# Last 128 tokens' values in two column halves, last transfers from two queues, low-word shift of the weights also on ScalarE, new order

## The chip, the cores and the metric

One core of one Trainium2 chip. The metric is the device time of one execution in microseconds (us): 916.03 us, the median of 3 runs (915.87 to 916.19).

The engines in the tables: PE is TensorE's matmul, PEld its weight load, DVE is VectorE, ACT is ScalarE, POOL is GpSimd, SP is SyncE, which here issues nearly all transfers. The names of lines (L459) are lines of the kernel before.

## The reference

Threshold attention, then a channel mix of the RWKV kind, all in fp32. There are 8 batches of 576 tokens, 8 heads of 64, so a model width of 512; the hidden width is 1024.

```python
scores = q @ k.T / 8
scores = where(scores >= max(scores) - tau, scores, -1e9)
x = softmax(scores) @ v                      # heads side by side: [8, 576, 512]
xk = mu_k * x + (1 - mu_k) * x_prev          # x_prev: the token before, zero at the start
xr = mu_r * x + (1 - mu_r) * x_prev
k = relu(xk @ w_k)                           # 512 -> 1024
out = sigmoid(xr @ w_r) * ((k * k) @ w_v)    # 1024 -> 512
```

q, k and v are fp32. The three weight matrices come as 64-bit floats, which the kernel takes as pairs of 32-bit words.

## The kernel before, in words

**An order written down.** The kernel first lists 5,647 steps. `add` records for each its engine, a cost, the code that issues it, and which buffers (or regions of them) it reads and writes. Some steps have alternatives on another engine (`alt`); the string `PICKS` says, step by step, which is taken. The table `PLACES` then gives every step its place in one global order, two digits for each. `follow` reads it and picks buffer slots; `issue` emits the steps in that order. Each engine runs its own steps in the order in which they were emitted, and semaphores hold a step until what it depends on is done. A step that waits therefore holds all later steps of its engine.

**Attention.** Per batch there are four pairs of heads; a pair of heads is a job (batch 0's jobs come in two halves). A job works in units of 128 query rows. Per unit and head PE writes the scores of 576 keys into PSUM (L628, L639, L656), DVE takes the maximum (L740), the threshold is made of it on ACT, DVE or POOL (L748, L756, L761), ACT takes the exponential (L768), DVE masks and sums (L776), DVE inverts the sum (L801), and ACT or POOL scales (L816, L812). The result is turned, by PE and an eviction from PSUM (L830, L845 on ACT, L846 on DVE) in the first two batches, by DVE and transfers after (L865, L878). Then PE multiplies with v (L1017), and an eviction puts x into place. For full precision operands are split into a high and a low part, and three products are summed.

**Weights.** There are 20 pieces of 128 x 512 (8 of w_k, 4 of w_r, 8 of w_v). `weight` turns the 64-bit words of a piece into fp32 and splits it, in the midst of the attention of the first batches. A piece takes a transfer (L435), a clamp of its high words on POOL (L444), a scaled copy on ACT (L451), then three steps on DVE that join in the low words' top bits: a shift right by 29 into a PSUM buffer (L459), sign bits joined to that (L467), and the final join (L477). A copy on ACT or POOL (L487, L491) and a difference on POOL (L496) make the two parts. The PSUM buffer is one of four of the tag `w`, which PE's matmuls and transposes use too.

**Mix.** `ffn_chunk` handles 256 tokens: 16 chunks of a batch's own (main) and 2 of four batches' last 64 tokens (end). It mixes neighbours, multiplies with w_k (L1211), applies relu and squares (L1219, L1220, L1224 or L1234, L1243), multiplies with w_r (L1262), takes the sigmoid through tanh (L1266, L1270 or L1273), multiplies with w_v (L1285), takes the product of both on DVE (L1291), and sends the rows out (L1301). The value product runs over two tiles of 128 tokens, each 8 slices of the hidden width with three matmuls of 512 columns. The last thing that the kernel does is the second such tile of the last end chunk: a product of 128 x 512, and two transfers of 64 rows each, both from SP.

```python
            add(
                "DVE",
                0.6,
                lambda j=j, vps=vps: V.tensor_tensor(sg.get()[:, j], vps.get(), sg.get()[:, j], op=ALU.mult),
                reads=[vps],
                writes=[(sg, j)],
                key=key - 20,
            )
            n = P // len(rows[j])
            for y, dst in enumerate(rows[j]):
                add("DMA", DQ, lambda j=j, y=y, dst=dst, n=n: SY.dma_start(dst, sg.get()[y * n : (y + 1) * n, j]), ...)
```

Of the kernel before, what the change touches and what calls it, by code (L numbers as in the profile page):

```python
# [22 lines left out]
    "!(!!!$!#!+!,!o%x!*!)!%!&!1!=!r!}$0$C$>$G$^%C%m!.!c!n#)#1#=#E#H!w#g$U&)&9&](Z(t!2!]#G#Q#a#w$M&>!0#b&4(*(9(B(S(~#+#m#v",  # L23
    "&p&y(%(z)+!`&Q)&)1)H)^*,*7#@$B(`(b(p({*(*A#L$;)w*4*D*N*T*b%[&J)s)f)y*%*9*Z!f$)*B*S*d*n*v*{$E&~*Y*y*~+)+0+8$])j*x+.+3",
    "+A+K+R!e#>+G+E+T+e-<-H$?&[,|.1.A.N.q/$#4$F+p,C,Q,X.E/Y%d(0+c+[+o+|,*,=(l+`-a-N-i-u-~.)#Z.4/T/M/]/e/j/o*)-e0$0*060<0G",
    "0L!-!P#l!>!<!C!E!F!Q!?!A!B!D!S!V!x#!!_!k!X!q!^#&!T!O![!b!d!j!U!W!Y!a!l!~#3#8!s##!y#(#-#0#:#I#N#d#h#p!@#,$Z!i!m!p!u!t",
    "!z!v!|!{#%#*#D#M#O#<#B#6#J#T#[#$#.#/#7#2#9#5#C#;#F#W#}$1$:$!$+#j#s#R#Y$J$N$O$S$V$[!/!R%W#A#U#K#V#P#X#`#f#c#i#{#~$I$T",
    "#n#x$($5$2$@#r#_#z$%$#$-#e#q#k#u$8$=$z$~$g$x$,$<$`$c%,%2%4%F%K%c!Z#?&<#S#]#t$9$4#|#o$$$.$6#y$D$K$H$P$&$3$/$7$Y${%+%B",
    "$p$t$l%8$k$n$A$X$L$R$Q$W$b$i$h$o%b%o%|&!$r%$%&%:%=%N&,&/&1&6&:&K$_%3%U%g*K%9%I%V&c()(8(^)T)q(J(i)S){*0*6*=*F*L*Q*U*W",
    "*e+D+m+r,),1,4,:,k,o,r,{-:-@.:.T*@*J*O*]*a*g*q*z+,+w-k.v-v-z-}.+.U.^.c.e.m.w/</C+4+;+>+M+V*u*|+(+C+Q,Y/Q/_/b/h0P0^0b",  # L30
    "1E1L1_0y0}1%11191G1u1{2%2T$*$e(3$m$w$}%#%(%E%S%@%L$a$d$f$j$s$q$u%7%<%M%]%f&$%}%j%p%s$v$y$|%%%!%-%*%0%)%1%.%5%?%G%P%_",
    "%r&&%T%`&E&G%>%D%6%;%H%X%R%Y%A%O%J%Q%n%v&i&l%l%w%~&?%e%k&x(#(&(-(/(T(Y%/%h))%{&+&0&H&X&T&2&8&B%Z%^%a%i%u%q%z&C&N&R&`",
    "&Z&g&d&k&n&u%t%y&%&(&#&*&-&3&.&5&7&=&f($(1(6&A&U&M&_&h&t&;&@&F&I&D&S&L&V&P&Y&W&b&q&z(A(X&{(2&s&|(](d(o(s(y(|)%);)=&O",
    "(()z(.(5(<(C(H(M(=(W(e&^&a&e&j&r&w(+(Q(v)>)L(I).(n(E(K(L(4(7&m&o(>(D(F(N&v&}(!(,(m(u)#),(_(g(:(?(j(x(V(a(;(@(h(q(r)$",
# [263 lines left out]
def tile_threshold_attention_then_rwkv_ffn(  # L298
# [1153 lines left out]
```

## Time and profile before

| | us |
|---|---|
| median of 3 runs | 916.03 |
| the profiled execution | 915.72 |
| its span, first to last instruction | 914.00 |
| PE busy | 902.3 |
| DVE busy | 715.5 |
| POOL busy | 666.5 |
| ACT busy | 598.5 |

The span is that of one profiled execution; the time around it is 1.72 us. Busy time counts an instruction from its start to its end, and instructions of one engine overlap a little, so the sum of single durations is larger than the busy time. In the chain of waits each piece stands only for the time until the next piece takes over, so there a group's pieces are shorter than its durations. A share of busy time is a mean over stages with different limits.

### The profile page before, as it was taken

How to read it: one execution, taken by the hardware profiler on the slowest of the kernel's cores; microseconds unless marked ns; L12 is line 12 of the kernel's file. 1: busy time of each engine (PE TensorE's matmuls, PEld its weight loads, DVE VectorE, ACT ScalarE, POOL GpSimd, SP SyncE). 2: the span in 40 equal slices, each digit the busy share in tenths (PEclk: the TensorE clock that was granted, in tenths of full speed). 3: DMA queues.
4: the chain of work that ended last, by engine and by line, in shares of the span. 5: the costliest groups of instructions: out<-in, count | busy, mean ns of one | idle time of the engine just before them, and what ended most of it. 6: DMA issues, size and time to landing. Idle time of an engine off the chain costs nothing.

```text
span 914.0 us, 17624 instructions
## 1 busy us (share of the span) xinstructions
PE 902.3 (99%) x5970; PEld 744.1 (81%) x5970; DVE 715.5 (78%) x1615; ACT 598.5 (65%) x1154; POOL 666.5 (73%) x824
## 2 busy tenths in 40 slices
PE   8999999999999999999999999999999999999997
PEld 6677877797878887988887978888889888879986
DVE  7999999998878898988889988888888777701131
ACT  6789999778675767565755475757686666434211
POOL 1789988886774967786977686867687868577742
PEclk9999999999999999999999999999999999999999
DMA  8767333499989999899987979999898887630001
GB/s 332 276 217 246 105 106 119 145 305 308 334 296 311 313 320 322 301 323 313 299 297 272 315 252 321 305 321 320 296 321 291 281 310 261 238 131 24 24 24 23
DMA packets 146249, 226.60 MB, mean 248 GB/s; under 512 B 20080, under 2 KB 82672, under 8 KB 146160
## 3 DMA queue, kind: packets, MB, share of 16 engines
q1 hardware_dynamic: 146016, 225.49, 73.1%
q8 instruction: 47, 0.77, 0.4%
q14 instruction: 42, 0.34, 0.1%
q10 hardware_dynamic: 144, 0.00, 0.0%
HBM read 108.27 MB, written 73.14 MB: 198 GB/s over the span
## 4 chain that ended last, share of the span: by engine, by line
PE 84%; DVE 9%; ACT 4%; issue 1%; POOL 1%; ACTq 0%; DVEq 0%; POOLq 0%
PE w L1211 21%; PE w L1285 20%; PE w L1017 15%; PE s L656 12%; PE w L1262 9%; DVE p L776 3%; DVE sm L740 3%; PE s L628 3%; PE w L830 2%; PE s L639 2%; ACT p L768 2%; ACT pm L845 1%; DVE pt L865 1%; PE w L1378 0%; DVE r L1161 0%
## 5 line engine op out<-in xcount | busy, mean ns | idle before, releaser
L768 ACT ACTIVATE p<-s,sm 128x576 f32<-128x576 f32 x288 | 209.6, 738 | 122.8 <-DVE sm L740 100.0
L776 DVE SCALAR_TENSOR_TENSOR p<-s,sm,p 128x576 f32<-128x576 f32 x288 | 230.9, 811 | 32.4 <-ACT p L768 19.7
L740 DVE TENSOR_REDUCE sm<-s 128x1 f32<-128x576 f32 x288 | 213.2, 750 | 42.4 <-PE s L656 30.4
L1211 PE MATMUL w<-xk,wk 128*128 128x256 f32 x1728 | 227.5, 281 | 0.0
L1211 PEld LDWEIGHTS w<-xk,wk 128*128 128x128 f32 x1728 | 215.8, 188 | 4.1 <-issue 1.7
L1285 PE MATMUL w<-wv,k 128*128 128x512 f32 x864 | 218.0, 395 | 0.0
L1285 PEld LDWEIGHTS w<-wv,k 128*128 128x128 f32 x864 | 157.6, 188 | 31.2 <-ACT raw L529 0.4
L1017 PE MATMUL w<-pm,v 128*64 128x256 f32 (+1 forms) x1280 | 164.9, 409 | 0.0
L1017 PEld LDWEIGHTS w<-pm,v 128*64 128x64 f32 x1280 | 88.1, 137 | 64.0 <-issue 5.8
L865 DVE STREAM_TRANSPOSE pt<-p 128x1024 f32<-128x1024 f32 x96 | 117.8, 1228 | 8.0 <-POOL p L812 5.0
L812 POOL TENSOR_SCALAR p<-p,sm 128x576 f32<-128x576 f32 x119 | 89.2, 753 | 39.0 <-DVE sm L801 36.7
L1243 POOL TENSOR_TENSOR k<-r,k 128x512 fp32r<-128x512 f32 x72 | 93.0, 1294 | 31.0 <-ACT k L1224 28.4
L816 ACT ACTIVATE p<-p,sm 128x576 f32<-128x576 f32 x133 | 101.3, 771 | 20.2 <-DVE sm L801 19.8
L1262 PE MATMUL w<-wr,xk 128*128 128x512 f32 x432 | 112.4, 395 | 0.0
L656 PE MATMUL s<-st 128*128 128x288 f32 x480 | 107.9, 308 | 1.9 <-DVE p L776 1.6
L567 POOL TENSOR_TENSOR hl<-raw,hl 128x640 fp32r<-128x640 f32 (+1 forms) x64 | 97.9, 1539 | 14.3 <-ACT hl L550 7.8
L656 PE MATMUL s<-st,st 128*128 128x288 f32 x480 | 102.2, 296 | 0.0
L656 PEld LDWEIGHTS s<-st 128*128 128x128 f32 x480 | 78.3, 189 | 20.4 <-DVE p L776 8.3
L1262 PEld LDWEIGHTS w<-wr,xk 128*128 128x128 f32 x432 | 77.5, 188 | 13.8
L656 PEld LDWEIGHTS s<-st,st 128*128 128x128 f32 x480 | 77.2, 188 | 1.9
L1220 ACT ACTIVATE r<-r 128x512 f32<-128x512 f32 x72 | 45.4, 631 | 34.8 <-DVE r L1219 33.7
L1291 DVE TENSOR_TENSOR sg<-w,sg 128x512 f32<-128x512 f32 x36 | 24.0, 680 | 44.8 <-PE w L1285 40.9
(93 smaller groups left out, 1129.3 us busy)
## 6 DMA issues: line engine op xcount, KB each, us to landing
far<-pt SPq DMA_DIRECT2D x96, 576.0 KB, 4.2
pm<-far SPq DMA_DIRECT2D x48, 1152.0 KB, 7.3
st<-hl SPq DMA_DIRECT2D x64, 288.0 KB, 3.9
raw<-in_qk SPq DMA_DIRECT2D x28, 640.0 KB, 5.0
st<-hl SPq DMA_DIRECT2D x56, 256.0 KB, 3.8
v<-in_v SPq DMA_DIRECT2D x36, 320.0 KB, 4.0
st<-hl SPq DMA_DIRECT2D x64, 144.0 KB, 3.3
out<-sg SPq DMA_DIRECT2D x32, 256.0 KB, 4.0
```

Source lines behind the costliest of these rows:

```text
L567: lambda cs=cs: G.tensor_tensor(hl.get()[:, 1, cs], raw.get()[:, cs], hl.get()[:, 0, cs].bitcast(F32), op=ALU.subtract),
L656: PE.matmul(ss[y].get()[:, z, 0:HS], l.get()[:, c * P : (c + 1) * P], r[:, z * HS : (z + 1) * HS], start=(j == 0), stop=(j == 1),)
L740: lambda sv=sv, col=col: V.tensor_reduce(col(0), sv(), axis=AX.XY, op=ALU.max, negate=True),
L768: lambda sv=sv, pv=pv, col=col: A.activation(pv(), sv(), AF.Exp, bias=col(0)),
L776: lambda sv=sv, pv=pv, col=col: V.scalar_tensor_tensor(pv(), sv(), col(1), pv(), op0=ALU.is_ge, op1=ALU.mult, accum_out=col(2)),
L816: alt=[("ACT", 0.667, lambda y=y: A.activation(half(y), half(y), AF.Copy, scale=sm.get()[:, 3, y : y + 1]))],
L865: V.transpose(o, x)
L1017: PE.matmul(o[g].get()[hs, 0 : n[g]], vt.get()[:, c, hs], pt, start=(c == 0), stop=(c == 4))
L1211: PE.matmul(h.get()[:, f], l, r, start=(ct == 0 and i == 0), stop=(ct == NCT - 1 and i == 2))
L1243: lambda r=r, js=js: G.tensor_tensor(k2.get()[:, 1, js], r.get().rearrange("p (a b) -> p a b", a=2), k2.get()[:, 0, js].bitcast(F32), op=A ...
L1262: PE.matmul(z.get(), l, r, start=(ct == 0 and i == 0), stop=(ct == NCT - 1 and i == 2))
L1285: PE.matmul(vps.get(), l, r, start=(ft == 0 and i == 0), stop=(ft == NFT - 1 and i == 2))
```

## The change

1. The last end chunk's second tile is made in two halves of 256 columns, each with its own PSUM buffer, its own 24 matmuls, its own DVE product and its own two transfers of 64 rows by 256 columns. Of the second half, the second transfer is issued from ACT's queue instead of SP's.
2. The shift of the low words (L459) gets an alternative on ACT: a copy that reads the words as integers, multiplies by 2^-29 x 0.936 and writes an integer. `PICKS` takes it for 18 of the 20 pieces.
3. `PLACES` and `PICKS` are new throughout: another global order (5,658 steps), and other choices of engine for many steps. Thresholds go 93 to 65 on ACT, 117 to 142 on DVE and 78 to 81 on POOL; scalings go 133 to 119 on ACT and 119 to 133 on POOL.

```diff
 PLACES = (
-    "!(!!!$!#!+!,!o%x!*!)!%!&!1!=!r!}$0$C$>$G$^%C%m!.!c!n#)#1#=#E#H!w#g$U&)&9&](Z(t!2!]#G#Q#a#w$M&>!0#b&4(*(9(B(S(~#+#m#v",
...
 W_SCALE = 2.0**-112
+L_SCALE = 2.0**-29 * 0.936
...
             reads=[(words, 0)],
             writes=[bits],
             key=key,
+            alt=[("ACT", 0.57, lambda: A.activation(bu(), words.get()[:, :, 0], AF.Copy, scale=L_SCALE))],
         )
...
     def ffn_chunk(kind, b0, g, key):
+        final = kind == "end" and b0 + NTB == B
...
+            parts = 2 if final and j == 1 else 1
+            for part in range(parts):
+                fs = slice(part * DM // parts, (part + 1) * DM // parts)
+                vps = psum("w", [P, DM], 4)
+                for ft in range(NFT):
+                    w = pieces["v", ft, 0]
+
+                    def mm(ft=ft, w=w, vps=vps, ts=ts, fs=fs):
+                        wt, x = w.get(), k2.get()
+                        prods = [(x[:, 0, ft, ts], wt[:, 0, fs]), (x[:, 0, ft, ts], wt[:, 1, fs]), (x[:, 1, ft, ts], wt[:, 0, fs])]
+                        for i, (l, r) in enumerate(prods):
+                            PE.matmul(vps.get()[:, 0 : fs.stop - fs.start], l, r, start=(ft == 0 and i == 0), stop=(ft == NFT - 1 and i == 2))
...
+                    lambda j=j, vps=vps, fs=fs: V.tensor_tensor(sg.get()[:, j, fs], vps.get()[:, 0 : fs.stop - fs.start], sg.get()[:, j, fs], op=ALU.mult),
+                    reads=[vps] if parts == 1 else [vps, (sg, j)],
+                    writes=[(sg, j) if parts == 1 else (sg, (j, part))],
...
+                n = P // len(rows[j])
+                for y, dst in enumerate(rows[j]):
+                    eng, q = ("ACT", A) if part and y else ("DMA", SY)
+                    add(
+                        eng,
+                        DQ if eng == "DMA" else 0.55,
+                        lambda j=j, y=y, dst=dst, n=n, fs=fs, q=q: q.dma_start(dst[:, fs], sg.get()[y * n : (y + 1) * n, j, fs]),
```

## Rows read from the trace of the kernel before

**Rows 1.** The head of the page.

```profile
span 914.0 us, 17624 instructions
PE 902.3 (99%) x5970; PEld 744.1 (81%) x5970; DVE 715.5 (78%) x1615; ACT 598.5 (65%) x1154; POOL 666.5 (73%) x824
```

**Rows 2.** Busy time by stretch; columns as the first line names them.

```profile
core 0: us, PE busy (x) PEld busy (x) DVE busy (x) ACT busy (x) POOL busy (x), PEclk, DMA share, GB/s
0.00:57.10 57.10, 54.34 (x361) 39.23 (x362) 48.75 (x119) 41.83 (x94) 32.20 (x52) 1.00 0.80 292
57.10:169.30 112.20, 109.77 (x803) 86.06 (x802) 109.30 (x257) 104.99 (x237) 98.44 (x120) 1.00 0.46 151
169.30:800.00 630.70, 628.84 (x4169) 525.00 (x4168) 537.05 (x1191) 418.58 (x767) 470.69 (x582) 1.00 0.89 298
800.00:914.00 114.00, 109.38 (x645) 93.79 (x643) 20.37 (x52) 33.14 (x56) 65.20 (x72) 1.00 0.14 44
```

**Rows 3.** Chain of waits, 57.1 to 169.3 us: shares; pieces (start, us, what).

```profile
by line: DVE sm L740 10.9%; DVE p L776 10.4%; PE w L1017 9.7%; PE w L830 9.2%; ACT p L768 8.1%; PE s L656 7.5%; ACT pm L845 7.2%; PE w L1211 4.5%; issue 4.4%; PE w L1285 3.7%; DVE w L467 3.3%; DVE xT L477 3.3%; DVE w L459 3.2%; PE s L628 2.
...
68.42 0.18 ACT sm L748
...
71.48 0.56 ACT xT L451
...
102.59 0.60 DVE w L459
...
111.35 0.14 DVE sm L756
...
116.23 0.66 ACT p L816
...
120.97 0.58 ACT xT L451
...
142.12 0.23 DVE pm L846
```

**Rows 4.** Chain of waits at the end, from 881 us (start, us, what).

```profile
881.35 9.87 PE w L1211 x84
...
898.23 11.16 PE w L1285 x48
909.39 0.02 issue
909.41 0.69 DVE sg L1291
```

**Rows 5.** Instruction groups, shapes apart: busy us, mean ns, idle before.

```profile
L1219 ACT ACTIVATE r<-w 128x512 f32<-128x512 f32 x49 | 29.1, 593 | 28.3 <-PE w L1211 26.5 <-POOL k L1243 1.5
L1291 DVE TENSOR_TENSOR sg<-w,sg 128x512 f32<-128x512 f32 x36 | 24.0, 680 | 44.8 <-PE w L1285 40.9 <-ACT sg L1270 3.8
L451 ACT ACTIVATE xT<-wk 128x512 f32<-128x512 f32 x8 | 5.5, 681 | 0.0
L1039 DVE TENSOR_TENSOR xT<-w,xT 128x256 f32<-128x256 f32 x8 | 3.4, 420 | 0.0
```

**Rows 6.** Timeline at the end: SP's last output transfers (start, us).

```profile
908.09 3.15 SPq L1301 DMA_DIRECT2D out<-sg  x4
```

**Rows 7.** Timeline of the first 14 us: start, us, engine and line.

```profile
0.73 0.40 ACTq L379 DMA_DIRECT2D small<-in_tau  x1
...
9.11 0.50 ACT L529 ACTIVATE k<-k,small 128x256 f32<-128x256 f32 x1
...
13.22 0.99 PE L639 MATMUL s<-k 64*128 64x288 f32 x3 [0.29 <-DVE p L776]
```

**Rows 8.** DMA issues: count, KB of each, median us to landing.

```profile
out<-sg SPq DMA_DIRECT2D x32, 256.0 KB, 4.0
...
out<-sg SPq DMA_DIRECT2D x8, 128.0 KB, 3.1
xk<-in_qa SPq DMA_DIRECT2D x2, 448.0 KB, 7.3
...
k<-in_qa SPq DMA_DIRECT2D x1, 448.0 KB, 4.8
```

**Rows 9.** Busy time from 450 to 500 us.

```profile
450.00:500.00 50.00, 48.62 (x321) 39.89 (x320) 44.22 (x104) 29.08 (x55) 36.65 (x47) 1.00 0.89 301
```

More of the change, by code (lines that the diff above doesn't have):

```diff
@@ new lines @@
+    "0m!.!S#O!;!=!>!D!A!E!C!G!H!T!U!X!c!o!_!g![!l!e#-!V!R!^!f!d!i!W!Y!Z!b!k!m!v!~!|#,!t!w!x#!#2#4#9#G#J#d!?#($Q!h!n!p!r!s",
+    "!y!u!}!{#$#7#T$)$,#M#X#i#s#<#]###)#+#6#.#8#3#D#:#E#H#b$&$.#g#j#m#y#k#x$3$5$E$J$L$S!<#U%X#A#Q#I#R#N#V#a#e#f#l$-$D$P$Z",
+    "#r#z$+$>$/$9#t#`#}$%$$$0#h#n#o#u$I$g$n%%$f$u$k$y$R$m%2%4%G%J%P%Z!]#%&A#*#;#B#F#p$4#Y#C#S$:#|$B$G$F$K$*$7$2$<$T$t%.%>",
+    "${%#$q$|$^$b$A$U$H$O$M$X$a$j$h$o%d%t%y%|%*%9%&%5%C%O&-&0&4&:&<&O$Y%@%M&G(^%[%i&V&`&q&z(/(p*U(&)*)O)u*&*+*-*9*F*H*M*O",
@@ new lines @@
+    "*Y+S+v,),2,6,:,m,p,v,w,z-D-r-z.#*Z*_*h*l*o*q*t*v+)+G.6.E-S-X-}.!.*.,...7.N.d/,/1+>+A+K+Q+h*~+(+9+H+Y1&/H/L/d/l0c0u1$",
+    "131U1h0{1?1D1p1v2%2*202K2Z#w$V(6$l%!$r%,$s%A%T%F%L$_$c$e$i$v$p$w%:%<&P&X%h&%%w%W%u%n$~%$$x$z%)%/%0%7$}%-%(%1%K%Q%V%e",
+    "&!&+&H&L%Y%_%?%D%8%;%H%S%U%a%B%N%I%R&)&3&W&d%p%x%v%~%l%q&}(#()(+(1(h(l%3%g)7%}&*&8&I&a&Y&2&9&N%]%b%c%k%s%r%z&&&,&?&D",
+    "&v(;(A&x&|(.%m%{&$&(&#&1&/&7&.&6&5&=&E&c(:(C&b&o&^&f&T&Z&K&M&@&C&S&_&]&e&J&Q&R&[(@(Q(Y(a&r&w(B(T&m&s(q(u(w),)0)<)>&U",
@@ new lines @@
+    "(0)t(5(?(H(I(=(V(N(D(]&g&h&k&{($(%(,(3(Z(o(z(G(b(e)$)2)-(4(7&n&y(<(K(F(M(!(-(*(2(t)A)F)J(j(y(J(O(_(~(S(W(9(>([(m(f(s",
+    "(E(P(L(R)&);)M)Z):)?)6)E)P)V)`*;*1(d)9+{)C)K)[)c)S)k)])N)h(`(c(g(n(x(v({)T)a){*!)X)o)m)}*6*2(})#)%)+)()1)/)5).)4)3)B",
+    "*%*/*Q*T)D)H)U)s*B*E)=)@)I)Q)R)n)^)q)Y)_)d)i***0*R*]*7*<*C*K*j*w+d,*+|-b*.,@,c,k,s-M-p.X/>/h/}1b2G2j0_111Y1l2^2{3&3*",
+    "353R3j3p3}4/464831323@3U3_3e3i3n4?4B4E4K2P2T2V2`2c2e2i2t2x33373K2l2o2r3$303F3J3W3Z3b3f3k3A3M3t3x3~4O4i5(565U5Y4T4s4y",
@@ new lines @@
+    "5!5/5=5C5G5l684Y4_4n595K5Q5V5]5f5m)y*g-a+#+F+T+O+s+n+f+i+`)r)v)z)~*4*,*5*a+$+M+]+t+e+b+x+u*=*?*#*3*D*W*P*X*>*I*G*N*d",
+    "*i*m*s*y+&+3+[+++6*b*e*V*[*p*z*x+%*c*{*n*|+;+D+^+l,/,;+y,%,.,4,F,b,Z+/+1+,+5+4+=+?+L+:+C+B+I+_+k+}+q,=,?,,,0,9,J+W+Z",
+    "+P+X+a+p+j+r+g,!,+,1,H,N,R,],Y,_,h,x,g,t-*-L,$,W/=,d,|-,-.,n-B-G-P-V+~,&,(,-,7,5,<,G,O,S,i-9-7,}-2--,>,A,B,E,D,K,L,Q",
+    ",I,T,P,U-!-0-6-=-@-H-F-O-Q-Y,a,e,[,`,j,q,r,y,f,o,l,u-5-8->-E-Z-c-`-h-R-e.H.c.Z,~-#-%-(-&-1-/-4-+-:-3-;-A-J-W-d-s-~-w",
@@ new lines @@
+    "./-k-o-<-?-I-N-C-K-U-]-T-_-[-g-m-x.%-{.2.O.1.@.=.A.|/:-^.80l.M.i._.}.w/6/%.V/+-l-q-v.$.3.+.4.?.C.F.a.p.r.`.n/&-f-i.&",
+    ".(-n-y-u-|.-.9.5.;.K.Q.U.T.e.t.g.k.o/3.<.>.B.G.D.I.L.S.J.R.].f.s.v/$.z/5/S/D/I/;/B/~050>.Y.^.u.y.b.j.h.l/!/-/(/./9/F",
+    "/J/O/[/c/Y/u/X/].m.q///2.x.~/#/*/7/@/E/K/R/V/a/Z/k0&/i/p/v/y020@/C/x2I0!0+03040,0a0]0e0w/8/</A/G/M/N/W/o0*0I0Z151,0X",
+    "0v0t/_/b/Q/T/e/q/j/r/`/f/g/m0$0(0:000B0J0G0S0F0H/z/|/s/w0#0/0-01/{0%07090=0A0D0C0K0P0`0p0N0U1P1o1}0<0?0O0R0E0M0L0Q0T",
@@ new lines @@
+    "0[0Y0b0h0|1%1#1;1e1-171:1M0V0W0q0s0^0g0d0i0x0}0~1(1L1T1s1`1~2+1g1j1{22272u2J2n4[5E6)3!3T3v3z4>4U4q5;5>4e4l4r5%6_6b6j",
+    "6n6q6y6z72777>7B7F5p5t636=6@6C6H6M6Q6X6^6c5h5j676I6R6Z6t767M7Q7X7]6e6i6w7#7(7,7C7O7j7t7y7~7G7J7Y7_7f7.7:7?7T7[7}828G",
+    "8K8P8T8j8q8~9*9G8-888>8B8]8a8g8u9/9i4R5P5a6$7|8D5g6B7a7e8&819!9;9T868A8Q8k9h9p:0:2:4:C:F:N:R:X:]:f9%9(9+919495989=9D",
+    "9V9W9g:+:7:<:A:H:K:`:a:m:s:y;#9.9f9m9t9x9{9~:#:-:1:::@:[:r:};(;3:U:d:i:w;0;w;7;;;[;^;j;|<#<0<L<r;1;n;t<-<8<=<C<J<]<c",
@@ new lines @@
+    "0;0k5&191E1N1y1]212<25280j0n0o0r0z0y1!1*1.10161@1=2k1d1t2U2N3%1)1+12181/141>1A1<1C1B1F1I1Q1[1^1f1n1r1J1O1G1H1R1_1V1a",
+    "1K1W1S1Z1w1z2&2$2,2>2B3+1i1k1c1m1q1|1x2#1u2(2!2)2.2=2@2D2W2d2g2-2/2426232;2:2A292E2?2F2M2Q2]2S2v2|3#3G4.5*4u4I1X2C65",
+    "2_3]2s3o2q3a3{3w4$2O2Y2[2a2m2h2p363B3E3L3V3S534}4f4Q5)4W2H2L2w2~2R2b2X2f3(3.3-343:3<3D3?3^3I3h2y2z3;3=2}3,3)3/3C3O3H",
+    "3P3`4%4,4)47454:4^38393c3d3>3N3Q3X3l3r3s3y4(4+41444G4=4P3Y3[3|4!3g3q3m3u4-4342494D4F4Z4d4o4t4w5@5w6V6A6}4<4j834~5.5H",
@@ new lines @@
+    "5W5y5S5[5`5u4#4&4*404@4;4A4C4a4|5+57516D6?6v6J60714H4J4L4M4N4X4V4]4S4b4`4g4v4z555,5A5L5M5-544c4h585?5<5D4k5#4x5$5_5q",
+    "5{5s6%6+6-6d4m4p5J5O4{50525:5T5^5Z5b5i5k5o5x6!5}6&5n5r5B5F5v6*6#6.5I5R5N5X62696<6K6S6]6a7)7k8|848v5|6[:)6s7L7$7`7N7R",
+    "7Z7W7s5c5d5e5z5~6(6,6N6f6x6~797<8(8.878H8r8=666:6/616>6L6G6O646E6;6F6U6k6|6r7E7-7K6W6Y6P6T6`6l6h6p6g6o6m6u6{737@787h",
+    "7n7r8L7!7&7%7+7*7=7/7A7075747;7c7m7p7o8#7u8,7D7S7H7I7b7l7x7{7P7U7V7^8$8*80858@8<8F8d9F;):g9a9N9Y9_;6<*9q;-;?;C;I;R;`",
@@ new lines @@
+    ";u<3;V;Z;g;o<e<u<|=+=1=?=A=D=[=_=q=w<h<j<m<o<{=4=8=:=C=H=M=T=$=.=l=p=r=v=y=}>!>*>1><<P<U<Y<Z<^<a<p<y<~=(=7=<=i>8>>>E",
+    ">J>)>.>3>g>k>|>Y>i?E?M?O?f?j?o@J@c>L>S>^?9?@?Z?^?c?h@9<_;y=G?.?G@3=O=Z>#>4>h>o>u>~?S?&?6?>?H@#@<@A@D@Q@^A*A7A?ACAGAK",
+    "@$@(@,@5@8@:@V@Y@]@q@u@y@aA5ABADAEAIAJAMASAXA^Ac?{?|@*@0@G@H@T@U@W@g@kA9A-AeAgAmB!A;AQAVB0BDC/A{B(B+B8ByC*C0C4C=DAAk",
+    "AsAyB>BCBtB|C#C7D#7w8C;m8M8X8b968l939R9O9K7d7g7i7q7v7z8!898:8?8^8w9::!9z:S:,9c:B8)8+8%8E8/8;8J8O8I8R8N8S8V8c8t8f978z",
@@ L135 @@
+    "10010011001000111110101101",
 )
 W_SCALE = 2.0**-112
+L_SCALE = 2.0**-29 * 0.936
 W_MAX = 2.0 ** (0x8F - 127) * (1 + 0x6FFFFF / 2.0**23)
@@ L1276, in ffn_chunk @@
             ts = slice(j * P, (j + 1) * P)
-            vps = psum("w", [P, DM], 4)
-            for ft in range(NFT):
-                w = pieces["v", ft, 0]
-                def mm(ft=ft, w=w, vps=vps, ts=ts):
-                    wt, x = w.get(), k2.get()
-                    prods = [(x[:, 0, ft, ts], wt[:, 0]), (x[:, 0, ft, ts], wt[:, 1]), (x[:, 1, ft, ts], wt[:, 0])]
-                    for i, (l, r) in enumerate(prods):
-                        PE.matmul(vps.get(), l, r, start=(ft == 0 and i == 0), stop=(ft == NFT - 1 and i == 2))
-                add("PE", 0.69, mm, reads=[w, *([k2] if ft == 0 else [(k2, (0, ft // 2)), (k2, (1, ft // 2))])], writes=[vps], key=key, lat=0.86)
@@ L1288, in ffn_chunk @@
-            add(
-                "DVE",
-                0.6,
-                lambda j=j, vps=vps: V.tensor_tensor(sg.get()[:, j], vps.get(), sg.get()[:, j], op=ALU.mult),
-                reads=[vps],
-                writes=[(sg, j)],
-                key=key - 20,
-            )
-            n = P // len(rows[j])
-            for y, dst in enumerate(rows[j]):
-                add(
-                    "DMA",
-                    DQ,
-                    lambda j=j, y=y, dst=dst, n=n: SY.dma_start(dst, sg.get()[y * n : (y + 1) * n, j]),
-                    reads=[(sg, j)],
+            parts = 2 if final and j == 1 else 1
@@ new lines, in ffn_chunk @@
+            for part in range(parts):
[8 more added lines that the diff above has]
+                            PE.matmul(vps.get()[:, 0 : fs.stop - fs.start], l, r, start=(ft == 0 and i == 0), stop=(ft == NFT - 1 and i == 2))
+                    occ = 0.69 if parts == 1 else 0.36
+                    add("PE", occ, mm, reads=[w, *([k2] if ft == 0 else [(k2, (0, ft // 2)), (k2, (1, ft // 2))])], writes=[vps], key=key, lat=occ + 0.17)
+                add(
+                    "DVE",
+                    0.6 if parts == 1 else 0.33,
+                    lambda j=j, vps=vps, fs=fs: V.tensor_tensor(sg.get()[:, j, fs], vps.get()[:, 0 : fs.stop - fs.start], sg.get()[:, j, fs], op=ALU.mult),
+                    reads=[vps] if parts == 1 else [vps, (sg, j)],
+                    writes=[(sg, j) if parts == 1 else (sg, (j, part))],
@@ L1303, in ffn_chunk @@
                     key=key - 20,
-                    kb=256 // len(rows[j]),
                 )
+                n = P // len(rows[j])
[5 more added lines that the diff above has]
+                        lambda j=j, y=y, dst=dst, n=n, fs=fs, q=q: q.dma_start(dst[:, fs], sg.get()[y * n : (y + 1) * n, j, fs]),
+                        reads=[(sg, j) if parts == 1 else (sg, (j, part))],
+                        key=key - 20,
+                        kb=256 // len(rows[j]) // parts,
+                        lat=None if eng == "DMA" else 2.4,
+                    )
```

182 lines of the change are left out of this document (73 added, 109 removed).

## The prediction

> **What bounds the kernel now.** I read the head of the page first: a span of 914.0 us with TensorE (PE) busy for 902.3 [rows 1]. That alone would say that only PE's own work counts. The stretches then split the span [rows 2]. From 169.3 to 800 us PE is busy for 628.84 of 630.70, so there other engines only feed it. Before 169.3 this is not so: from 57.1 to 169.3, where most of the 20 weight pieces are unpacked beside the softmax, VectorE (DVE) is busy for 109.30 of 112.20 (2.9 idle) and ScalarE (ACT) for 104.99 (7.2 idle). PE's 109.77 counts each matmul with its latency, so it hides gaps. The chain of waits in that stretch shows who holds it up [rows 3]: the named DVE lines add up to 31% (maxima 10.9, masks 10.4, and the three bit steps of the weights 3.3, 3.3 and 3.2), the named ACT lines to 15% (8.1 and 7.2), and PE's to 35% (9.7, 9.2, 7.5, 4.5, 3.7). The shift of the low words, L459, is one of those bit steps. Last I read the end: from 881 us on the chain holds nothing but PE's own work, and after the last matmul stand one DVE product of 0.69 us and then output transfers [rows 4]. So two places can give time: the unpacking stage and the tail. The granted clock is 1.00 in every stretch [rows 2], so the clock has no part in this.
>
> **The tail, step by step.** The profiled execution took 915.72 us, 1.72 more than its span; its median stands 0.31 above it, so a change worked out in the span is carried to the median unchanged (the forecast is a span of 911.6, a profiled execution of 913.3). The end has these terms:
> - PE. 24 matmuls of 512 columns become 48 of 256. By the chain, 48 of 512 took 11.16 us (0.2325 each), and 84 of 256 took 9.87 (0.1175 each) [rows 4]. So 48 x 0.1175 - 24 x 0.2325 = **+0.06 us**. The order now also finishes tokens 0 to 127 before the last 128, all on one full engine: nothing.
> - DVE. The last product shrinks from 512 columns (680 ns) to 256; the nearest row is L1039, a product with PSUM of 256 columns at 420 ns [rows 5]: **-0.26**. The first half's product runs under the second half's 24 matmuls (2.8 us).
> - Issue. The last product was followed by two transfers from SP one behind the other; four such issues took 3.15 us with a wait among them [rows 6], and the ACT queue issued its only one in 0.40 [rows 7]. Now the second goes out from ACT at the same moment as the first from SP. ACT has nothing queued behind it by then. Bounds: 0 (both share the engines that move the bytes) to 0.6; I take **-0.5**, a whole issue. The first half's two transfers from SP are issued 2.8 us earlier and are out of the way.
> - Bytes. Each last transfer falls from 128 to 64 KB. Output transfers of 256 KB took 4.0 us to land and those of 128 KB 3.1 [rows 8]; halving again could give up to 0.45, or nothing where the rest is fixed. I take **-0.2**.
>
> Together **-0.9 us**, bounds -0.2 and -1.25. The rule against this part is in the Trainium skill, "DMA: Bandwidth & Descriptors", under its rules for kernel authors: under 64 KB a transfer is mostly overhead, and splitting into two that share the 16 engines is not worth it; by its fit (a fixed 2.0 us plus bytes) the halving would give 0.15 us, an estimate, and the sum would move by 0.05. No row here shows a 64 KB output.
>
> **The unpacking stage.** I counted both order tables against the program's list of steps: how many instructions of each kind stand between the 25th and the 73rd maximum (L740), which the trace has at 57.1 and 169.3 us. Prices are the slots that the chain's pieces show [rows 3].
> - DVE: shifts 16 to 2, -14 x 0.60 = -8.4; thresholds (L756) 14 to 29, +15 x 0.13 = +1.9; evictions (L846) 13 to 20, some 0.2 each = +1.4; one reciprocal less, -0.1. Net **-5.2**.
> - ACT: shifts 0 to 15. No row shows ACT reading or writing integers, or writing these words to PSUM. The nearest row is L451, an ACT copy of 512 elements out of the same buffers with the same stride of two words, at 681 ns [rows 5], a slot of 0.56 to 0.58 in the chain; below it stands L1219 at 593. I take 0.57, with 0.48 as the lower bound (L1219 less the same overlap) and twice 0.57 as the upper, if the stride or the conversion should cost double. +15 x 0.57 = +8.6. Thresholds (L748) 22 to 6, -16 x 0.18 = -2.9; scalings (L816) 14 to 11, -3 x 0.66 = -2.0; evictions 92 to 85, -1.4; the rest +0.3. Net **+2.6**.
> - GpSimd (POOL): three scalings more, other things less, under +1 in all, with 13.8 us idle there [rows 2]: nothing.
>
> Two estimates of what this gives. By shares of the chain: 0.31 x 5.2 - 0.15 x 2.6 = 1.2 us. By the fuller engine: ACT's 105.0 + 2.6 with DVE's present 2.9 us of idle is 110.5 instead of 112.2, so 1.7 at most; DVE alone would allow 5.2. Before 57.1 the order has 1.2 us less DVE work and 0.3 more of ACT, but there DVE is idle for 8.3 of 57.1 [rows 2]: 0.2. I take **-1.5 us** for all of it; bounds -5.4, and +6.9 if the shift costs double (below).
>
> The Trainium skill's page "ScalarE: Activation LUTs" (rules for kernel authors) speaks against the move: plain arithmetic belongs on VectorE, and an ACTIVATE is budgeted at about 0.3 us plus 0.83 ns per element. That makes an estimate of 0.73 us for 512 elements, where L451 shows 0.68; the stage would give 0.1 us less.
>
> **Moved and waiting steps.** The shift now waits on ACT for its words and for one of four PSUM buffers; behind it stand the exps (L768) and evictions (L845), and the masks on DVE wait for those exps. Before, the same wait stood on DVE. I price it inside the shares above. On SP's queue the load of the second head pair's operands (k<-in_qa) now goes behind two weight loads; with 1.9 MB ahead it should land as the xk loads do, 7.3 us after an issue near 2.6, so near 10, and ACT's scaling of it, at 9.11 before, waits up to 0.9 us. The scores that need it ran at 13.22 [rows 7, 8]: nothing, and 0.9 if that cover goes. After 169.3 the table gives ACT some 12 us less, POOL 9 more, DVE 2 more; PE is full there, and POOL is idle for 160 us [rows 2]: nothing. Between 450 and 500 us PE lacks 1.4 us [rows 9]; a new order may close that or open another: 0, bounds -1.4 and +1.4.
>
> Sum: -0.9 - 1.5 = **-2.4 us**: 916.03 becomes **913.6**.
>
> **Rivals.** About 0.2% (1.8 us) is what a measurement of this kernel tells from no change.
> - *The stage gives nothing* (chance 0.26): ACT takes on 15 instructions in a stretch where it has only 7.2 us idle, so the chain moves from DVE to ACT and stays as long. For it: ACT's net rises. Against it: DVE is on the chain twice as often as ACT. Then only the tail is left: 916.03 - 0.9 = 915.1.
> - *The whole DVE relief comes through* (0.12): the new order lets ACT work where it was idle. 5.2 + 0.2 + 0.9 gives 909.7. Against it: ACT would need to be fuller than DVE is now.
> - *ACT's shift is dear, slower than before* (0.07). With a slot of 1.14 instead of 0.57, ACT needs 107.6 + 8.6 = 116.2 of work and 2.9 of idle, 119.1 against 112.2: +6.9, less the tail's 0.9, 922.0. It decides from a slot of about 0.86 on, where 1.8 us are lost over all. Against it: L451 reads the same stride at a slot of 0.57.
> - *The change does not do what it says* (0.05): both last transfers land no earlier, as they share their engines, and the stage does not move: 916.0.
>
> **How the numbers follow.** My forecast has 0.50: a gain of 1.5 to 4 us, 912.0 to 914.5, nearly all of it beyond the 0.2%. The range 910.2 to 915.6 adds the first rival and about half of the second; outside stay the dear shift, the null case and half of the full relief, 0.18. Faster: 0.48 + 0.12 = 0.60. Within 0.2%: 0.26 + 0.05 + 0.02 = 0.33. Slower: 0.07.
>
> **What would show it.** Right: 18 ACT instructions on the shift's line near 0.6 to 0.7 us; DVE busy for some 104 us between the same two maxima and that stretch some 1 to 2 us shorter; a last product near 0.42 us, and 3.6 us from the last matmul to the span's end instead of 4.6. Wrong: a mean over 0.95 us on the shift's line; ACT's lines named ahead of DVE's in the stage's chain with the stretch unchanged; or PE short of full somewhere after 169 us by more than before.

## The result, and the profile after

The changed kernel took **922.50 us** (median of 4 runs, 921.03 to 925.02) against 916.11 for the kernel before in the same measurement (4 runs, 915.87 to 916.19). The ratio is 1.0073 [1.0049, 1.0097]: slower by 0.7%, where 913.6 was forecast, with a range up to 915.6. The profiled execution took 921.6 us with a span of 919.8, 5.8 us more than the span before.

The head of the page of the changed kernel answers to [rows 1]:

```profile
span 919.8 us, 17676 instructions
PE 906.7 (99%) x5994; PEld 746.3 (81%) x5994; DVE 715.3 (78%) x1623; ACT 595.0 (65%) x1138; POOL 677.8 (74%) x833
```

DVE has as much to do as before and ACT 3.5 us less; POOL has 11.3 more. No engine's total explains 5.8 us. The windows by stage, with the columns of [rows 2], bounded by the changed kernel's own 25th and 73rd maximum (L742 here; behind the shift the line numbers are 2 to 9 above those of before):

```profile
0.00:57.50 57.50, 55.11 (x359) 39.52 (x360) 47.61 (x122) 42.66 (x93) 32.39 (x53) 1.00 0.81 293
57.50:170.40 112.90, 110.46 (x802) 85.95 (x801) 106.56 (x264) 106.92 (x232) 99.87 (x119) 1.00 0.43 149
170.40:800.00 629.60, 624.83 (x4113) 519.16 (x4112) 537.53 (x1184) 407.28 (x748) 478.77 (x590) 1.00 0.88 295
800.00:919.80 119.80, 116.25 (x726) 101.68 (x724) 23.61 (x56) 38.15 (x66) 66.75 (x72) 1.00 0.19 61
```

Two things stand against [rows 2]. The unpacking stage lasts 112.9 us instead of 112.2, although DVE's work in it fell from 109.30 to 106.56: DVE is now idle for 6.3 us there (2.9 before) and ACT for 6.0 (7.2 before). And from there to 800 us PE lacks 4.8 us of being full, where it lacked 1.9. The clock is 1.00 throughout, so it has no part in this. The chain of waits in the unpacking stage, which DVE's lines led before [rows 3], is now led by PE's own, and neither DVE nor ACT stands out in it:

```profile
by line: PE w L1019 19.1%; PE s L658 15.8%; PE w L832 14.9%; DVE p L778 7.9%; ACT p L770 5.8%; DVE sm L742 4.8%; PE w L1214 3.7%; PE s L630 3.7%; PE w L1291 3.3%; ACT w L464 2.7%; DVE xT L479 2.7%; PE w L680 2.4%; issue 2.0%; ACT pm L847 2.
```

**Where PE lost the time.** Both kernels give PE the same work, so I compared them at equal work: each matmul counts with the distance from its start to the next one's where nothing holds it up (0.2325 us for 512 columns, 0.1175 for 256), and the time that has passed less this sum is what PE has lost so far. Worked out from the matmul records of each trace, in us:

```
PE work done        50    100    120    150    200    440    480    520    872
before           11.22  16.63  19.90  21.93  24.43  28.74  31.25  31.77  36.28
changed          11.48  17.07  19.45  23.98  26.43  32.07  37.48  38.29  43.08
```

The changed kernel is 0.45 us ahead at 120 and 2.05 behind at 150 (span time 140 to 172 us); 1.3 more go in small amounts up to 440; 2.9 go between 440 and 480, 0.6 after that. That makes 6.8 at the last matmul. The tail gives back 1.1, which leaves about the 5.8.

**The loss between 440 and 520.** PE's waits from 435 to 520 us (waiter, waited for, us, times, longest), in the changed kernel and then in the one before:

```profile
PE s L658 <- DVE p L778: 3.9, 2, 2.2
PE s L658 <- DVE xT L848: 0.3, 1, 0.3
```

```profile
PE s L656 <- DVE p L776: 1.4, 1, 1.4
```

Scores (PE) wait for masks (DVE), twice instead of once. The timeline of the changed kernel shows what stands ahead of those masks on DVE, and a block of the same instructions with no POOL instruction beside it (501.27):

```profile
487.33 1.29 POOL L1246 TENSOR_TENSOR k<-r,k 128x512 fp32r<-128x512 f32 x1
...
487.48 4.29 DVE L1164 SCALAR_TENSOR_TENSOR m<-m,mu_sb,xE 128x64 f32<-128x64 f32 x8
...
489.03 1.69 POOL L569 TENSOR_TENSOR hl<-raw,hl 128x640 fp32r<-128x640 f32 x1
...
492.06 0.82 DVE L778 SCALAR_TENSOR_TENSOR p<-s,sm,p 128x576 f32<-128x576 f32 x1
...
492.94 0.54 PE L658 MATMUL s<-st 128*128 128x288 f32 x2 [1.70 <-DVE p L778]
...
501.27 1.64 DVE L1164 SCALAR_TENSOR_TENSOR r<-m,mu_sb,xE 128x64 f32<-128x64 f32 x8
...
508.89 5.21 DVE L1164 SCALAR_TENSOR_TENSOR m<-m,mu_sb,xE 128x64 f32<-128x64 f32 x8
...
508.91 1.57 POOL L569 TENSOR_TENSOR hl<-raw,hl 128x640 fp32r<-128x640 f32 x1 [1.34 <-ACT sm L798]
...
510.46 1.05 POOL L1276 TENSOR_SCALAR sg<-sg 128x1024 f32<-128x1024 f32 x1
...
511.47 1.56 POOL L569 TENSOR_TENSOR hl<-raw,hl 128x640 fp32r<-128x640 f32 x1
...
514.95 0.53 PE L658 MATMUL s<-st 128*128 128x288 f32 x2 [2.16 <-DVE p L778]
```

L1164 is the neighbour mix of an end chunk: eight small instructions in a row, one for each batch and half. The tile of these instructions (duration ns min/median/max, first and last start), changed kernel and then before:

```profile
L1164 DVE SCALAR_TENSOR_TENSOR r<-m,mu_sb,xE x16: 268/280/685, 480.4 to 502.6; 128x64 f32<-128x64 f32 x16
L1164 DVE SCALAR_TENSOR_TENSOR m<-m,mu_sb,xE x16: 272/274/1677, 487.5 to 513.8; 128x64 f32<-128x64 f32 x16
```

```profile
L1161 DVE SCALAR_TENSOR_TENSOR r<-m,mu_sb,xE x16: 274/281/1301, 485.8 to 500.4; 128x64 f32<-128x64 f32 x16
L1161 DVE SCALAR_TENSOR_TENSOR m<-m,mu_sb,xE x16: 246/275/696, 491.7 to 503.1; 128x64 f32<-128x64 f32 x16
```

Most take 275 ns, some up to 1677. The long ones end within 0.1 us of the end of the POOL instruction beside them: of the eight from 508.89 on, the first three take 1677, 1080 and 1619 ns, as long as L569, L1276 and L569 (1.57, 1.05 and 1.56 us), and the other five the usual time. The block at 501.27, with no POOL instruction beside it, took 1.64 us for eight. The kernel before has such blocks too; its longest:

```profile
485.75 4.16 DVE L1161 SCALAR_TENSOR_TENSOR r<-m,mu_sb,xE 128x64 f32<-128x64 f32 x8
```

From 480 to 515 us each kernel has four blocks. What they take beyond 1.64 us each adds up to 3.7 us before (blocks of 4.16, 2.04, 1.65 and 2.44) and to 6.7 in the changed kernel (2.11, 4.29, 1.64 and 5.21): 3.0 more, beside the 2.9 that PE lost more between 440 and 480 of its work.

L1164 is this kernel's only DVE instruction that reads two whole tiles in SBUF (m and xE; mu_sb is one value for each row). The mask L778, with one whole tile in SBUF (p), one value for each row (sm) and the scores in PSUM, shows no such spread in the changed kernel:

```profile
L778 DVE SCALAR_TENSOR_TENSOR p<-s,sm,p x288: 773/817/821, 8.4 to 800.9; 128x576 f32<-128x576 f32 x144
```

The Trainium skill, "SBUF — State Buffer" (section "Who interferes with whom"), says that a DVE instruction with two SBUF inputs contends with a GpSimd instruction that reads SBUF, and calls the shared pair of ports an exclusive lock. The 1677 ns against 274 agree with it.

**The loss between 120 and 150** looks different: many short waits. Waits from 140 to 172 us: the weight loads', DVE's and ACT's longest in the changed kernel, then the weight loads' in the one before:

```profile
PEld s L658 <- DVE p L778: 3.3, 7, 0.8
...
DVE p L778 <- ACT p L770: 0.8, 2, 0.6
...
ACT sm L798 <- DVE p L778: 1.1, 1, 1.1
...
ACT p L770 <- DVE sm L742: 1.0, 3, 0.5
```

```profile
PEld s L656 <- DVE p L776: 0.5, 1, 0.5
```

The scores wait for masks, DVE's masks for ACT's exps, and ACT for DVE's maxima and sums: each step of a unit waits a little for the one before it. What makes these waits is not shown by this list.

**The parts of the change that were priced.** Instruction groups (busy us, mean ns), shapes apart:

```profile
L464 ACT ACTIVATE w<-wk 128x512 uint32<-128x512 uint32 x8 | 5.2, 656 | 0.0
L464 ACT ACTIVATE w<-wv 128x512 uint32<-128x512 uint32 x6 | 3.8, 638 | 0.1
L464 ACT ACTIVATE w<-wr 128x512 uint32<-128x512 uint32 x4 | 2.6, 656 | 0.0
L1298 DVE TENSOR_TENSOR sg<-w,sg 128x256 f32<-128x256 f32 x2 | 0.9, 426 | 4.5 <-PE w L1291 4.5
```

The shift on ACT takes 0.64 to 0.66 us, a little less than L451's 681 ns [rows 5], and the half product takes 0.43. The end of the timeline, and the issues of output transfers (count, KB, median us to landing):

```profile
916.29 0.43 DVE L1298 TENSOR_TENSOR sg<-w,sg 128x256 f32<-128x256 f32 x1 [2.35 <-PE w L1291]
916.80 0.55 ACTq L1309 DMA_DIRECT2D out<-sg  x1
```

```profile
out<-sg SPq DMA_DIRECT2D x3, 64.0 KB, 2.0
out<-sg ACTq DMA_DIRECT2D x1, 64.0 KB, 2.2
```

From the last product to the span's end stand 3.5 us (916.29 to 919.8) where 4.6 stood [rows 4].

### The profile page after: what moved, and what is told of

Its sections match the earlier page's. It is cut to its first block, busy times and chain, and to the rows that moved or that the text cites. A ratio compares the mean times of both kernels' runs of the same rounds, so it can differ in the third digit from the quotient of the medians.

```text
span 919.8 us, 17676 instructions
## 1 busy us (share of the span) xinstructions
PE 906.7 (99%) x5994; PEld 746.3 (81%) x5994; DVE 715.3 (78%) x1623; ACT 595.0 (65%) x1138; POOL 677.8 (74%) x833
## 4 chain that ended last, share of the span: by engine, by line
PE 88%; DVE 6%; ACT 4%; issue 1%; POOL 0%; DVEq 0%; ACTq 0%; POOLq 0%
PE w L1214 21%; PE w L1291 20%; PE w L1019 16%; PE s L658 14%; PE w L1265 10%; PE w L832 3%; PE s L630 3%; DVE p L778 2%; DVE sm L742 1%; ACT p L770 1%; PE s L641 1%; DVE m L1164 1%; PE w L1387 1%; PE w L680 1%; ACT pm L847 0%
## 5 line engine op out<-in xcount | busy, mean ns | idle before, releaser
L778 DVE SCALAR_TENSOR_TENSOR p<-s,sm,p 128x576 f32<-128x576 f32 x288 | 231.0, 810 | 29.5 <-ACT p L770 15.1
L742 DVE TENSOR_REDUCE sm<-s 128x1 f32<-128x576 f32 x288 | 212.6, 749 | 48.4 <-PE s L658 36.7
L1291 PE MATMUL w<-wv,k 128*128 128x512 f32 (+1 forms) x888 | 220.4, 389 | 0.0
L814 POOL TENSOR_SCALAR p<-p,sm 128x576 f32<-128x576 f32 x133 | 99.3, 751 | 39.7 <-DVE sm L803 36.6
L569 POOL TENSOR_TENSOR hl<-raw,hl 128x640 fp32r<-128x640 f32 (+1 forms) x64 | 97.8, 1538 | 8.9 <-DMA pm<-end 3.3
L818 ACT ACTIVATE p<-p,sm 128x576 f32<-128x576 f32 x119 | 90.5, 771 | 14.0 <-DVE sm L803 13.8
L1222 ACT ACTIVATE r<-w 128x512 f32<-128x512 f32 x49 | 29.2, 596 | 45.4 <-PE w L1214 36.3
```

The lines of the kernel that those rows point to most:

```text
L569: lambda cs=cs: G.tensor_tensor(hl.get()[:, 1, cs], raw.get()[:, cs], hl.get()[:, 0, cs].bitcast(F32), op=ALU.subtract),
L742: lambda sv=sv, col=col: V.tensor_reduce(col(0), sv(), axis=AX.XY, op=ALU.max, negate=True),
L778: lambda sv=sv, pv=pv, col=col: V.scalar_tensor_tensor(pv(), sv(), col(1), pv(), op0=ALU.is_ge, op1=ALU.mult, accum_out=col(2)),
L814: lambda y=y: G.tensor_scalar(half(y), half(y), sm.get()[:, 3, y : y + 1], 0.0, op0=ALU.mult, op1=ALU.add),
L1291: PE.matmul(vps.get()[:, 0 : fs.stop - fs.start], l, r, start=(ft == 0 and i == 0), stop=(ft == NFT - 1 and i == 2))
```

## The experiments

Nine kernels, timed against the kernel before on the same chip. Its median was 916.05 in the measurement of the first four, 916.7 in that of the next three, 916.41 in that of the last two. Four build on the kernel before, five on the changed one.

**1. The tail alone.** The order and picks of before, with the last tile in two halves (for that tile alone the order is extended).

```diff
+            parts = 2 if final and j == 1 else 1
+            for part in range(parts):
...
+                    eng, q = ("ACT", A) if part and y else ("DMA", SY)
```

> The kernel before in its own order, with only the last tile in two column halves and its last transfer from ACT. Theory (the tail is sound, the loss is in the new order): about 1.0 us faster than before, 915.1, with the span after the last matmul 1.0 us shorter and PE's gaps elsewhere as before. Rival (the tail's gain is owed to the new order's arrangement): no change or slower, 916.0 to 916.5.

915.73 us, ratio 0.9996 [0.9987, 1.0004]: -0.4 us, between -1.2 and +0.4. The median lies between what the theory and the rival expect. The profiled execution is one of the slower ones (916.63); the timeline of its end and its last transfer:

```profile
910.09 0.42 DVE L1296 TENSOR_TENSOR sg<-w,sg 128x256 f32<-128x256 f32 x1 [2.42 <-PE w L1289]
910.60 0.55 ACTq L1307 DMA_DIRECT2D out<-sg  x1
```

```profile
out<-sg ACTq DMA_DIRECT2D x1, 64.0 KB, 3.1
```

Product and issue are as in the changed kernel, but here the last 64 KB took 3.1 us to land and not 2.2, and the span ends 4.8 us after the product began. The tail gave 1.1 us in the execution of the changed kernel above and nothing in this one; the landing scatters by as much, so its gain can't be told from none.

**2. The shift alone.** The order of before; the same 18 shifts go to ACT.

```diff
+            alt=[("ACT", 0.57, lambda: A.activation(bu(), words.get()[:, :, 0], AF.Copy, scale=L_SCALE))],
```

> The kernel before in its own order, with only the 18 shifts moved from DVE to ACT. Theory (the move itself is harmless, the order costs): within 1.5 us of before, 914.5 to 917.5, and no new gap of PE after 200 us. Rival (the move costs, as it puts 0.54 us on ACT in front of exps and evictions): 3 to 7 us slower, 919 to 923, with PE's added gaps between 60 and 170 us.

922.51 us, ratio 1.0067 [1.0054, 1.008]: the rival's range, so the move by itself costs. The window between the 25th and 73rd maximum, and the shares of the chain of waits in it:

```profile
57.80:175.30 117.50, 111.94 (x799) 85.63 (x799) 103.07 (x244) 111.66 (x251) 97.79 (x119) 1.00 0.43 143
```

```profile
by line: ACT p L770 16.0%; ACT pm L847 11.6%; DVE p L778 8.4%; DVE sm L742 6.5%; ACT w L464 5.2%; PE w L832 4.8%; PE s L658 4.6%; PE w L1019 4.3%; ACT p L818 3.4%; issue 3.4%; ACT xT L452 3.3%; PE w L1287 3.0%; ACT sm L750 2.6%; ACT raw L53
```

The stage takes 117.5 us instead of 112.2. DVE's work falls by 6.2, ACT's rises by 6.7 to 111.66, and ACT's lines now lead the chain where DVE's did [rows 3]. ACT is now plainly the fuller engine, with 5.8 us of idle beside its work. A sum as in the prediction (ACT's 105.0 before, 15 shifts of 0.57 and 2.9 of idle: 116.5) comes near the 117.5 by two errors against each other: the work rose by 6.7 and not 8.6, and the idle time is 5.8 and not 2.9.

**3. The new order with the shifts back on DVE.** The changed kernel, its 18 picks of ACT for the shift undone (the edit of `PICKS` in words).

```diff
-shift of 18 pieces: pick 1 (ACT)
+shift of 18 pieces: pick 0 (DVE)
```

> The changed kernel in its new order, with the 18 shifts back on DVE. Theory (the order costs): still 3 us or more over before, 919 to 926, since the gaps near 490 and 512 us do not depend on the shift. Rival (the move costs): back to about 915 to 917.

930.25 us, ratio 1.0152 [1.0139, 1.0166]: slower even than the theory's 919 to 926, which looked only at the gaps near 490 and 512 us. The window of the stage:

```profile
58.90:178.20 119.30, 112.71 (x796) 85.44 (x796) 114.24 (x277) 100.50 (x218) 99.02 (x119) 1.00 0.41 141
```

Now DVE is the full engine (114.24 of 119.3). Runs 2 and 3 show one thing from both sides: the new order is made for the shift on ACT and the old one for the shift on DVE. The move alone costs 6.5 us; the new order in this stage takes that back (thresholds, scalings and evictions go from ACT to DVE and POOL), and no gain is left over.

**4. The changed kernel with the end-chunk mix joined.** One DVE instruction over four batches (256 columns) in the first end chunk, over 64 and 192 columns in the second, in place of four of 64. Same operands, same columns, fewer instructions.

```diff
-                            for o, n, _, prv in segs():
+                            for a, z in cuts:
+                                e = (b0 + a) % NE
                                 V.scalar_tensor_tensor(
-                                    d.get()[:, y, o : o + n],
+                                    d.get()[:, y, a * ST : z * ST].rearrange("p (b s) -> p b s", s=ST),
...
-                                    prv[:, hc + y],
+                                    xE.get()[:, hc + y, e : e + z - a, 0:ST],
```

> The changed kernel, with the mixing steps on DVE of the two end chunks (four instructions of 64 columns each, two SBUF operands) joined to one instruction over four batches in the first chunk and two in the second: 16 instructions of the first chunk's 32 x 2 blocks remain at a quarter of the count. Theory (these instructions wait for GpSimd's instruction in progress, and that makes PE's gaps near 490 and 512 us): the two gaps of 1.9 and 2.3 us shrink to under 0.5 each, 917.5 to 919. Rival (the gaps come from the order of the softmax alone): 921 to 923 as the changed kernel.

918.21 us, ratio 1.0025 [1.0015, 1.0034], 4.3 us below the changed kernel's median (the kernel before stood at nearly the same in both measurements, 916.05 and 916.11). The same block in its timeline:

```profile
507.56 3.06 DVE L1167 SCALAR_TENSOR_TENSOR m<-m,mu_sb,xE 128x256 f32<-128x256 f32 x2
507.58 1.58 POOL L569 TENSOR_TENSOR hl<-raw,hl 128x640 fp32r<-128x640 f32 x1 [1.33 <-ACT sm L798]
...
509.12 1.23 POOL L1279 TENSOR_SCALAR sg<-sg 128x1024 f32<-128x1024 f32 x1
...
511.47 0.30 PEld L658 LDWEIGHTS s<-st 128*128 128x128 f32 x2 [0.46 <-DVE p L778]
```

Two instructions can each be stopped once, so the block takes 3.06 us and not 5.21, with the same POOL work beside it. Not all of that is fewer stops: with no POOL instruction beside them the two take 0.88 us (at 500.10) where eight took 1.64. PE's matmuls show no wait in the list from 435 to 520 us, and PE loses 2.1 us between 440 and 520 of its work instead of 6.2. The joined instruction still waits (up to 1876 ns, where it takes some 480 with no POOL instruction beside it).

**5. The changed kernel with one operand instead of two.** The same number of instructions over the same columns, as transposes of 32 x 32 blocks with a single input. The multiply and the add of the mix are left out, so the results for the last 64 tokens of each batch are not the reference's.

```diff
-                                V.scalar_tensor_tensor(
-                                    d.get()[:, y, o : o + n],
...
+                                V.transpose(d.get()[:, y, o : o + n], diff.get()[:, y, o : o + n])
```

> The changed kernel, with each of the two end chunks' mixing steps on DVE (two SBUF operands, 64 columns) replaced by a 32x32 transpose of one SBUF operand, same count and columns; it leaves out the multiply and the add of that mix, so the last 64 tokens of each batch are not the reference's. Theory (an instruction with two SBUF operands waits for GpSimd's instruction in progress, one with a single operand does not): no such instruction over 0.4 us, where they reached 1.7 before, and PE's gaps near 490 and 512 us under 0.5 each; 917 to 919. Rival (the count or the place of these steps in DVE's order makes the gaps): 921 to 923, gaps as in the changed kernel.

917.38 us, ratio 1.0008 [0.9998, 1.0018]. The tile and the timeline at the same place:

```profile
L1164 DVE STREAM_TRANSPOSE r<-m x16: 201/204/225, 482.6 to 503.1; 128x64 f32<-128x64 f32 x16
L1164 DVE STREAM_TRANSPOSE m<-m x16: 201/203/242, 489.7 to 510.2; 128x64 f32<-128x64 f32 x16
```

```profile
509.29 1.11 DVE L1164 STREAM_TRANSPOSE m<-m 128x64 f32<-128x64 f32 x8
509.31 1.58 POOL L569 TENSOR_TENSOR hl<-raw,hl 128x640 fp32r<-128x640 f32 x1 [1.34 <-ACT sm L798]
```

Eight instructions again, beside the same L569, and none of the 32 takes over 242 ns: eight in 1.11 us instead of 5.21. A shorter instruction can account for 0.5 of that (1.64 undisturbed); the rest is the stops. So neither the number of instructions nor their place in the order is enough for POOL to stop them. The run drops two operands, xE and the row's value mu_sb; the mask L778 above keeps such a value and is not stopped, so it is the second whole tile in SBUF that matters.

**6. The kernel before with the mix joined.** The edit of run 4 in the kernel before.

> The kernel before, with the mixing steps of the end chunks on DVE joined over batches (one instruction of 256 columns for four of 64 in the first chunk). Theory (the same wait costs the kernel before 1.6 us near 490): 1.5 to 2.5 us faster, 913.5 to 914.6. Rival (only the new order meets it): 915.5 to 916.5.

913.95 us, ratio 0.9965 [0.9952, 0.9977]; in the trace 1.8 us less (914.0 to 912.2), 1.6 of it by 480 us of PE's work. The kernel before paid for the same stops; the new order, with its blocks beside more POOL work, paid more.

**7. The best of both.** The order of before, the tail of the change, the joined mix, and all shifts on DVE.

> The kernel before in its own order, with the tail in two column halves and the joined mixing steps, and the shifts left on DVE. Theory (the two gains add up): 0.3 to 1.0 from the tail and 1.5 to 2.5 from the joined steps, 912.7 to 914.3. Rival (the tail's gain is within the scatter of the last transfer's landing and does not add): 913.5 to 914.6, as the joined steps alone.

**913.81 us**, ratio 0.9967 [0.9956, 0.9979]: faster than both kernels, and in the range of the theory as of the rival. Beside run 6 the tail adds nothing that can be told.

**8 and 9. What is left between 120 and 150.** Run 4 still loses as much there as the changed kernel (24.40 at 150 against 21.93 before). The new order puts 29 thresholds on DVE in the stage instead of 14, and 15 of them leave DVE idle for some 0.1 us before the mask that needs them. Run 8 gives those 29 to POOL, run 9 to ACT, both on top of run 4 (again in words).

```diff
-29 thresholds from the 25th to the 73rd maximum: pick 1 (DVE)
+run 8: pick 2 (POOL); run 9: pick 0 (ACT)
```

> The changed kernel with the joined end-chunk mix (918.21 us, 2.1 us lost by TensorE between 120 and 150 us of its own work against the kernel before), and the 29 thresholds that VectorE makes between the 25th and the 73rd maximum given to GpSimd. Theory A, the thresholds put on VectorE hold up the masks right behind them (15 of the 29 leave VectorE idle for 0.1 us each before the mask): VectorE has some 6 us less to do there, the idle time behind thresholds goes, TensorE loses 1 to 2 us less by 150 us of its work, and the time is 916.5 to 917.5. Theory B, GpSimd's long instructions (1.2 to 1.6 us) stand before the thresholds, so that masks wait for GpSimd: 3 us or more is lost, 921 or more. Theory C, the order of all the steps sets the waits and not one group of them: within 1 us of 918.2.

> As the run before, but the 29 thresholds go to ScalarE. Theory A, VectorE is what holds this stage: some 6 us less on VectorE gives 1 to 2 us, 916.5 to 917.5. Theory B, ScalarE is the fuller one: 29 x 0.18 = 5.2 us more on ScalarE, which has 6.0 us of idle there, takes 2 to 4 us, 920 to 922. Theory C, the order of all the steps sets the waits: within 1 us of 918.2.

925.60 us, ratio 1.0111 [1.0084, 1.0138], and 922.48, ratio 1.0066 [1.0051, 1.0081]: theory B both times (run 9 half a us beyond its range). The waits of DVE in the stage and its window, run 8:

```profile
DVE p L778 <- POOL sm L763: 11.5, 15, 1.8
```

```profile
57.80:177.00 119.20, 112.02 (x802) 86.08 (x800) 102.74 (x234) 107.36 (x233) 106.58 (x149) 1.00 0.41 142
```

And run 9:

```profile
DVE p L778 <- ACT sm L750: 8.5, 17, 0.8
```

```profile
57.80:174.90 117.10, 112.18 (x801) 85.83 (x800) 102.99 (x234) 111.07 (x261) 99.68 (x119) 1.00 0.41 144
```

DVE has some 3.5 us less to do in both, and the stage gets 4 to 6 us longer than run 4's 112.8. A threshold of 0.2 to 0.3 us has to wait on the other engine behind what stands there, and the mask waits with it, up to 1.8 us. So taking the thresholds off DVE wins nothing back in this order. What in the new order costs the 2 us at 120 to 150, and the 1.3 up to 440, was not found. The end-chunk mix is not it, as run 4 loses as much there; whether the thresholds on DVE have a part in it stays open, as runs 8 and 9 bring longer waits of their own.

## Why the prediction was wrong

**What held.** What bounds the kernel: an unpacking stage that DVE and ACT hold up, PE elsewhere, and a tail. The tail's terms: the half product at 0.43 us (0.42 forecast), the two issues side by side, 3.5 us to the end (3.6 forecast); the sum of -0.9 is the -1.1 of the trace of after, though run 1 shows that the landing's scatter swallows it. The Trainium skill, "DMA: Bandwidth & Descriptors" (rules for kernel authors), says not to bother with two transfers to disjoint partition halves, as they share the same engines; run 1's interval, from -1.2 to +0.4 us, holds both no gain and my -0.9, so it does not decide. The page's fit, which the prediction used beside its own term, is given there for transfers issued from GpSimd; these go out from SP and ACT and took 2.0, 2.2 and 3.1 us. The price of the shift on ACT: 0.64 to 0.66 us, so the dear-shift rival is refuted. That its 922.0 stands near the measured 922.5 is chance; none of the loss comes by its mechanism.

**The step that failed first: "I take -1.5 us for all of it".** The counts were right in kind: DVE's busy time in the stage fell (by 2.7 us, where the slots gave 5.2), ACT's rose (by 1.9; 2.6 forecast). But both ways of making a time of it assumed that idle time stays as it is. The "fuller engine" took DVE's 2.9 us of idle over to ACT. In no changed order did it stay so small: the fuller engine was idle for 5.8 us in run 2 (ACT) and for 5.1 in run 3 (DVE). In the changed kernel neither is the fuller: 106.6 and 106.9 of 112.9, and each is idle for about 6 us, in part because they wait for each other (140 to 172 us, above). Levelling two engines took 2.7 us from the fuller one and gave 3.4 of idle back. The rival "the stage gives nothing" came near the stage's length (112.9 for 112.2), but not by its mechanism: the chain did not move to ACT. By PE's work the stage cost more than this 0.7 us, as PE also had some 1 us less of its work behind it at the 73rd maximum, by the same matmul records. For the stage, -1.5 should have been about +2; what makes the waits stays open.

**The step that failed worst: "After 169.3 ... nothing" and "Between 450 and 500 us ... 0, bounds -1.4 and +1.4".** I had seen PE's 1.4 us gap [rows 9] and not asked what made it. It was the end chunk's mix, stopped by POOL (the 1301 ns above); with that known, the new order's table could have been searched for such blocks beside long POOL instructions. Runs 4, 5 and 6 settle it: joining gives 4.3 us in the changed kernel, a single tile as input removes the stops altogether, and joining helps the kernel before as well. The bounds were the size of the gap that was there; they had to be that of the mechanism, a POOL instruction's length (up to 1.7 us) for each of the eight that meets one.

**The sum.** Against the forecast span of 911.6 the trace shows 8.2 us more: some 3.5 by 150 us of PE's work (+2.05 where -1.5 stood), 4.7 after it (+4.75 where nothing stood; 2.9 of that at the two blocks), and the tail as forecast. The slower rival named one mechanism and it was another; the sign "PE short of full somewhere after 169 us by more than before" is the one that came true.

## What to carry to other kernels

A gap of 1 to 2 us on a full engine is worth following to the single instruction behind it before anything is reordered around it; here a group whose longest instruction took about five times its median gave 2 to 3 us, by joining four instructions into one, where the whole change lost 6. Moving work, in a fixed order, to an engine that is already busy for 88% or more of a stage can cost more, by what it makes wait there, than it gives back (runs 2, 8 and 9), so price it by what stands ahead of it there; levelling alone gave nothing here. A new order of the whole program is a change in every stage: each place where the old one had a gap needs a bound of its own, from the mechanism.

## What was not expected of the hardware

- A DVE instruction with two inputs in SBUF is held up by a POOL instruction in progress: 274 ns became up to 1677, and some 480 up to 1876 for the joined one. With one input it is not: 201 to 248 ns over all 64, beside the same kind of POOL work.
- The landing of a last 64 KB transfer scattered between executions of the same tail: 2.2 and 3.1 us, as much as the whole tail was worth.
- An ACT copy of integer words with a stride of two into PSUM (638 to 656 ns for 512 columns) costs no more than one of fp32 values (681 [rows 5]).
